# Nine key blocks instead of ten in the product with the values: the leftover 64 keys stand twice in one transposed block

## The chip, the cores and the metric

One core of a Trainium2 chip runs the whole program in one launch. The metric is the device time of that launch in microseconds (us); smaller is better. A core has five engines that run at the same time, each through its own queue in order: TensorE (PE, its weight loads shown apart as PEld), VectorE (DVE), ScalarE (ACT), GpSimd (POOL) and SyncE (SP, which here issues DMAs).

## What is computed

Three layers follow each other: a sharpened attention over 4 batches of 8 heads (576 tokens, head size 64), a gated MLP (512 to 1536 and back) and a squared-ReLU MLP (512 to 2048 and back) over the 2304 tokens. The change touches only the attention:

```python
scores = scale * np.matmul(q, k.transpose(0, 1, 3, 2))
thresh = np.max(scores, axis=-1, keepdims=True) - tau
scores = np.where(scores >= thresh, scores, -1000000000.0)
attn = np.exp(scores - np.max(scores, axis=-1, keepdims=True))
attn = attn / (np.sum(attn, axis=-1, keepdims=True) + 1e-09)
return np.matmul(attn, v)
```

## The kernel before, in words

**Number format.** Most matrix products run in a reduced format (f32r) on operands split in two: a high part (the rounded value) and a low part (what the rounding left). A product of two split operands is the sum of three or more matmuls.

**Tiles of the attention.** Queries go in tiles of 128 against all 576 keys: 9 tiles for each pair of heads, 4 pairs for each batch, 4 batches, so 144 tiles (`tiles`, `NTILE`). Two heads share the fifth tile (`ORDER`, kind "T"). The steps of a tile t are small functions, and the main loop (the last `for i in range(NTILE + lag + 1)` ahead of `at.close()`) calls the steps of several tiles in iteration i, `lag` being 2:

- `QK` (L653, PE): scores into one of two PSUM areas. `RED` (L663, DVE): row maximum less tau. `CUT` (L671, ACT): the thresholded scores into `z`. `EXP` (L679, ACT): the exponential into a tile `e` of 577 columns with its row sum; there are three `e` tiles in turn (`es`).
- `RCP` (L684, DVE) and `NORM` (L689, POOL), one iteration later: the reciprocal of the sum, and the 576 columns of `e` multiplied by it in place.
- `TR` (L711, PE), at i = t + 2: `e` is transposed by 128 x 128 matmuls with the identity, five blocks of keys for one tile. 576 keys are four blocks of 128 and one of 64. Bank `tx` takes keys 0 to 127, 128 to 255 and, as its third block, the 64 keys from 512 on; bank `ty` takes keys 256 to 383 and 384 to 511. From tile 20 on the attention has two PSUM banks for this, so tile t + 1 writes the same two banks that tile t wrote.
- `PH` (L731, ACT), at i = t + 3: the high parts, `tx` (384 columns) and `ty` (256 columns) into slots 0 to 4 of the tile `pt` (10 slots of 640 query columns). `PL` (L76, DVE): the low parts, bank less high part, into slots 5 to 9, with one subtraction for `tx` and one for `ty`. Both banks come free for the next `TR` when `PL` has read them.
- `AV` (L756, PE): the product with the values. For each pair of heads there are four products over query columns (`PARTS`: 256, 320, 320 and 256 columns, made at tiles 1, 4, 6 and 8 of the nine). Each is ten matmuls into one bank: five blocks of high parts and five of low parts, each against the 128 value rows of its block; the stationary operand has the high and the low parts of the values side by side, so that one matmul makes both products. The block of 64 keys is a full matmul whose lower 64 value rows are zero (`pack` puts zeros there), and the lower 64 rows of its block in the bank are zeroed once, by three `memset`s at the start (L432).

The first batch (`cfg["way"][0]`, letters D and K) goes another way: the transposed blocks are copied whole and the product is five plain f32 matmuls (L751, `ptf`, `vf`). It has no `PL` work. So `AV` at L756 is made for 12 pairs of heads: 48 products, and `PL` for 108 tiles.

**What else fills PE.** While the attention runs, `work(i)` gives PE matmuls of the first MLP for batches that are done (`fill_group`: L256 and L301), 12 of them in most iterations in which no product with the values is made.

**What sets the order.** Every engine takes its instructions in the order of a priority: the place at which the instruction is emitted in the program, moved up or down by `tc.high_priority(offset=...)`. `at_` takes the offset from `cfg["early"]` (from the second batch on): `TR` is moved 8 places ahead, `PL` 12 back, `NORM` 25 back, `PH` 6 ahead. In an iteration `QK` of the next tile is emitted, then `work(i)` (a product with the values, or fill), then `TR`; so the transposes stand among the last matmuls that `work(i)` emitted. The block of 64 keys has a further offset of 9 in `TR` and goes second.

The functions that the diff touches:

Of the kernel before, what the change touches and what calls it, by code (L numbers as in the profile page):

```python
# [10 lines left out]
F32 = mybir.dt.float32  # L11
F32R = mybir.dt.float32r
# [5 lines left out]
AF = mybir.ActivationFunctionType  # L18
ALU = mybir.AluOpType
# [3 lines left out]
P = 128  # L23
B, H, S, D = 4, 8, 576, 64
# [3 lines left out]
NPAIR = H // 2  # L28
# [15 lines left out]
SLOPE = 2.0**96  # L44
# [38 lines left out]
def attention_moe(tc, qkv, qk0, tau, w1, w2, out, cfg):  # L83
    nc = tc.nc
    ops = Ops(nc)
    mm = nc.tensor.matmul
# [334 lines left out]
    for j in range(LIVE):  # L421
        c0 = LAST + j * PIECE
# [5 lines left out]
    psum = p1.enter_context(tc.tile_pool(name="psum", bufs=1, space=PSUM))  # L428
    bank = [psum.tile([P, 512], F32, name=f"bank{j}") for j in range(4)]
    mp1 = Mm(bank[3:])  # L430
    for x in bank[:3]:
        nc.vector.memset(x[S - 4 * P :, 2 * P : 3 * P], 0.0)  # L432
    at = ExitStack()
    rawp = at.enter_context(tc.tile_pool(name="rawp", bufs=1, side="right"))
    qp = at.enter_context(tc.tile_pool(name="qp", bufs=2, side="right"))
    ptp = at.enter_context(tc.tile_pool(name="ptp", bufs=1, side="right"))

    es = [ptp.tile([P, S + 1], F32, name=f"e{j}", tag=f"e{j}") for j in range(cfg["lag"] + 1)]
    zs = [ptp.tile([P, S + 1], F32, name=f"z{j}", tag=f"z{j}") for j in range(cfg["zs"])]
    st_ = ptp.tile([P, S], mybir.dt.bfloat16, name="st_")  # L440
    sm = at.enter_context(tc.tile_pool(name="sm", bufs=4, side="right"))
# [7 lines left out]
    for i in range(2):  # L449
        t = [ptp.tile([P, P], F32R, name=f"qt{i}{j}", tag=f"qt{i}{j}") for j in range(2)]  # L450
# [30 lines left out]
    for h in range(4):  # L481
        c0 = 5 * 640 + h * (VW + D) + (1 - h % 2) * VW
        nc.gpsimd.memset(flat[:, c0 : c0 + D], 0.0)

    def whole(p, i):

        ways = cfg["way"][p // NPAIR % len(cfg["way"])]
        return p < NPAIR and ways[i] in "FEKD"
# [136 lines left out]
    SLOT = (0, 1, 4, 2, 3)  # L625
# [4 lines left out]
        6: (320, 320, 1, [(512, 0, 64), (256, 64, 256)]),  # L630
        8: (0, 256, 1, [(0, 0, 256)]),
    }
    pt = ptp.tile([P, 10, 640], F32R, name="pt", tag="pt")
    tiles = [(b, p, i) for b in range(B) for p in range(NPAIR) for i in range(9)]
    NTILE = len(tiles)
    st = [dict() for _ in range(NTILE + 8)]
# [38 lines left out]
    def EXP(t):  # L675
        e = es[t % len(es)]
        st[t]["e"] = e
        sum_ = sm.tile([P, 1], F32, name=f"sum{t}", tag="sum")
        ex = nc.scalar.activation(e, st[t]["z"], AF.Exp, scale=-SLOPE, accum_out=sum_)  # L679
        st[t].update(sum=sum_, exp=ex.ins)  # L680

    def RCP(t):
# [1 line left out]
        nc.vector.reciprocal(r, st[t]["sum"])  # L684

    def NORM(t):
        e = st[t]["e"][:, :S]
        r = st[t]["r"]
        norm = nc.gpsimd.tensor_scalar(e, e, scalar1=r, scalar2=1.0, op0=ALU.mult, op1=ALU.mult)  # L689
        st[t]["norm"] = norm.ins  # L690


# [4 lines left out]
    def way(t):  # L697
        b, p, i = tiles[t]
        return WAYS[cfg["way"][b % len(cfg["way"])][i]]

    def TR(t):
        e = st[t]["e"]
        tx, ty = (
            bank[(2 * t + j) % (3 if t < cfg["three"] else 2)][:, : n * P].rearrange("p (c q) -> p c q", q=P)
            for j, n in enumerate((3, 2))
        )
        for dst, cols in ((tx, ((0, 0), (2, 4 * P), (1, P))), (ty, ((0, 2 * P), (1, 3 * P)))):
            for j, c0 in cols:
                n = min(P, S - c0)
                with tc.high_priority(offset=9) if n < P else nullcontext():  # L710
                    mm(  # L711
                        dst[:n, j],
                        e[:, c0 : c0 + n],
                        ident,
                        is_transpose=True,
                        start=(j == 0),
                        stop=(j == 1),
                    )
        st[t].update(tx=tx, ty=ty)

    def halves(t):

        return ((st[t]["tx"], 0, 3, way(t)[0]), (st[t]["ty"], 3, 2, way(t)[1]))
# [8 lines left out]

    def PL(t):
        o = PTCOL[tiles[t][2]]
        for src, s0, n, how in halves(t):
            lo = pt[:, 5 + s0 : 5 + s0 + n, o : o + P]
            hi = pt[:, s0 : s0 + n, o : o + P].bitcast(F32)
            if how == "V":
                ops.sub("D", lo, src, hi)

    def AV(t):
        b, p, i = tiles[t]
        lo, n, odd, segs = PARTS[i]
        hd = heads[b * H + 2 * p + odd]
        no, o = mp1.tile()
        mr = slice(D, P) if odd else slice(0, D)
        cr = slice(0, D) if odd else slice(D, P)
        one = whole(b * NPAIR + p, i)
        if one:
            for k in range(5):  # L750
                mm(o[:, :n], hd["vf"][:, SLOT[k] * D : SLOT[k] * D + P], ptf[:, k, lo : lo + n], start=(k == 0), stop=(k == 4))  # L751
                if k < 4:
                    yield
        else:
            for k in range(10):
                mm(o[:, :n], hd["vs"][:, SLOT[k % 5], :], pt[:, k, lo : lo + n], start=(k == 0), stop=(k == 9))  # L756
        base = b * S
        out_x = [(xF[mr, p, base + dst : base + dst + w], slice(src, src + w)) for dst, src, w in segs]

        def main():  # L760
            for x_, sl in out_x:
                ops.copy("A" if not one else cfg["om"], x_, o[mr, sl])
            if one:
                end()

        def fin():
            for x_, sl in out_x:
                nc.vector.tensor_tensor(x_, x_, o[cr, sl], op=ALU.add)  # L768
            end()

        def end():
            if i == 8 and p == NPAIR - 1:
                fstate["done"] = b

        if one:
            mp1.post(no, (cfg["om"], main))
        else:
            mp1.post(no, ("A", main), ("D", fin))
# [92 lines left out]
    lag = cfg["lag"]  # L871
# [12 lines left out]
    for i in range(NTILE + lag + 1):  # L884
        mp1.age += 1
        fstate["i"] = i
        t = i - lag - 1
# [10 lines left out]
        if i < NTILE:  # L898
            at_(EXP, i)
# [3 lines left out]
        if 0 <= t < NTILE:  # L903
            at_(PL, t)
            if tiles[t][2] in PARTS:
                avq.append(t)
        if 0 <= i - 1 < NTILE:
            at_(RCP, i - 1)
            at_(NORM, i - 1)
# [5 lines left out]
        if 0 <= i - lag < NTILE:  # L915
            at_(TR, i - lag)
# [9 lines left out]
        if i < NTILE:  # L926
            b, p, k = tiles[i]
# [25 lines left out]
    f = 0  # L953
# [638 lines left out]
def pack(inputs):  # L1592
    import numpy as np

    q, k, v = (np.asarray(inputs[n]) for n in "qkv")
    qkv = np.zeros((B * NPAIR, P, RAWW), np.float32)
    qkv[:, :, 0:S] = q.reshape(B * NPAIR, 2, S, D).transpose(0, 1, 3, 2).reshape(-1, P, S)
    qkv[:, :, S : 2 * S] = k.reshape(B * NPAIR, 2, S, D).transpose(0, 1, 3, 2).reshape(-1, P, S)
    vv = v.reshape(B * NPAIR, 2, S, D)
    full = qkv[:, :, 2 * S :].reshape(B * NPAIR, P, 2, 5, D)  # L1600
    full[:, :, :, :4] = vv[:, :, : 4 * P].reshape(B * NPAIR, 2, 4, P, D).transpose(0, 3, 1, 2, 4)
    full[:, :D, :, 4] = vv[:, :, 4 * P :].transpose(0, 2, 1, 3)
    qkv[:, :, 2 * S :] = full.reshape(B * NPAIR, P, 2 * VW)

    def bits(w):
        return np.ascontiguousarray(w).view(np.int64)

    def cols(w, nf):
        return bits(w).reshape(NC, P, nf, P).transpose(2, 1, 0, 3).reshape(nf, P, DM)

    w1 = np.concatenate(
        [
            cols(inputs["moe_w_gate"], NF1),
            cols(inputs["moe_w_val"], NF1),
            bits(inputs["moe_w_out"]).reshape(NF1, P, DM),
        ],
        axis=2,
    )
    w2 = np.concatenate([cols(inputs["moe2_w_in"], NF2), bits(inputs["moe2_w_out"]).reshape(NF2, P, DM)], axis=2)
    tau = np.broadcast_to(np.asarray(inputs["tau"]).reshape(1, 1), (P, 1))  # L1620
    return [
        ("in_qkv_dram", np.ascontiguousarray(qkv)),
        ("in_qk0_dram", np.stack([np.concatenate([qkv[0, r : r + D, : 2 * S]] * 2) for r in (0, D)])),
        ("in_tau_dram", np.ascontiguousarray(tau)),
        ("in_w1_dram", np.ascontiguousarray(w1)),
        ("in_w2_dram", np.ascontiguousarray(w2)),
    ]
# [41 lines left out]
def program(arrays):  # L1669
    import concourse.bacc as bacc  # L1670

    nc = bacc.Bacc("TRN2", target_bir_lowering=False, num_devices=1, dynamic_dma_scratch_size=512)
    args = [nc.dram_tensor(n, a.shape, mybir.dt.from_np(a.dtype), kind="ExternalInput").ap() for n, a in arrays]
    out = nc.dram_tensor("out_0_dram", (NT, DM), F32, kind="ExternalOutput").ap()
    with tile.TileContext(nc) as tc:
        attention_moe(tc, *args, out, CFG)
    return nc
# [9 lines left out]
```

## Time and profile before

| what | us |
| --- | --- |
| time before, median of 3 runs | 1131.31 (1129.37 to 1132.91) |
| profiled execution, its own time | 1130.32 |
| span of that execution, first to last instruction | 1128.5 |
| PE busy | 1106.4 (98% of the span) |
| PE weight loads busy | 1007.2 (89%) |
| DVE busy | 848.8 (75%) |
| ACT busy | 677.0 (60%) |
| POOL busy | 240.6 (21%) |

The span is 1.8 us shorter than the profiled execution's own time, and that execution is 1.0 us below the median of the runs. Attention runs from the start to 418 us, together with fill; from then on only the two MLPs run. The ends of matmuls in a trace are modelled, so that a matmul of 0.12 us is drawn as 0.3 us long; the distance from one start to the next is what a matmul takes.

### The profile page before, as it was taken

To read this page: it belongs to the slowest core of one execution; us is meant where nothing else is said; L and a number is where in the kernel's file an instruction comes from. 1 tells how busy PE (TensorE), PEld (TensorE's weight loads), DVE (VectorE), ACT (ScalarE), POOL (GpSimd) and SP (SyncE) were. 2 spreads that over 40 slices of the span, in tenths; PEclk is the share of its full clock that TensorE was granted. 3 is DMA by queue.
4 is the path that set the end of the run, shared out by engine and by line. 5 is a ranking of instruction groups with operands and counts; after the bars stand their busy time and mean duration, and the time that the engine had idled before them with its cause. 6 is when DMAs were issued, how large, how long until landed. Compare 5 with 4: busy or idle time off the path is not lost.

```text
span 1128.5 us, 19599 instructions
## 1 busy us (share of the span) xinstructions
PE 1106.4 (98%) x6542; PEld 1007.2 (89%) x6542; DVE 848.8 (75%) x2088; ACT 677.0 (60%) x1593; POOL 240.6 (21%) x365
## 2 busy tenths in 40 slices
PE   7999999999999999999999999999999999999998
PEld 6788999999999999988888888888888998898887
DVE  7889987878787864889886878687568678866554
ACT  7889988988888872555434344245456455643321
POOL 5566765545455521000000000000000000000000
PEclk9999999999999999999999999999999999999999
DMA  7767645454444301222210234254355455443552
GB/s 210 218 187 197 172 118 125 113 130 119 109 108 108 76 1 47 86 94 84 76 56 20 95 129 159 95 212 180 132 195 187 168 172 183 162 160 119 193 175 78
DMA packets 60388, 148.08 MB, mean 131 GB/s; under 512 B 10240, under 2 KB 11520, under 8 KB 60288
## 3 DMA queue, kind: packets, MB, share of 16 engines
q1 hardware_dynamic: 60144, 146.83, 42.1%
q8 instruction: 52, 0.85, 0.3%
q14 instruction: 48, 0.39, 0.1%
q10 hardware_dynamic: 144, 0.00, 0.0%
HBM read 93.06 MB, written 22.28 MB: 102 GB/s over the span
## 4 chain that ended last, share of the span: by engine, by line
PE 74%; DVE 7%; ACT 5%; DMA 3%; issue 2%; POOL 0%; POOLq 0%; ACTq 0%; DVEq 0%; SPq 0%
PE mm L1497 17%; PE mm L256 16%; PE mm L1444 13%; PE mm L301 8%; PE bank L256 5%; PE bank L301 4%; PE bank L756 4%; PE bank L711 4%; PE s L653 3%; DMA wr<-in_w_dram 2%; ACT z L671 1%; DVE st__106 L663 1%; DVE pt L76 1%; ACT pt L731 1%; ACT e L679 1%
## 5 line engine op out<-in xcount | busy, mean ns | idle before, releaser
L711 PE MATMUL bank<-ident,e 128*128 128x128 f32 (+1 forms) x720 | 145.4, 276 | 3.5 <-ACT x L68 1.6
L689 POOL TENSOR_SCALAR e<-e,r 128x576 f32<-128x576 f32 x144 | 113.0, 785 | 123.7 <-DVE r L684 87.0
L76 DVE TENSOR_TENSOR pt<-bank,pt 128x384 fp32r<-128x384 f32 x216 | 100.5, 485 | 48.1 <-ACT pt L731 46.7
L256 PE MATMUL mm<-xs,wa 128*128 128x512 f32 (+2 forms) x672 | 125.8, 347 | 0.5 <-ACT x L68 0.5
L256 PEld LDWEIGHTS mm<-xs,wa 128*128 128x128 f32 x672 | 109.5, 188 | 15.7 <-ACT x L68 0.7
L671 ACT ACTIVATE z<-s,thr 128x576 f32<-128x576 f32 x144 | 106.7, 741 | 24.1 <-DVE st__106 L663 16.0
L663 DVE TENSOR_SCALAR_CACHE_REDUCE st__106<-s,tau_c 128x576 bf16<-128x576 f32 x144 | 116.8, 811 | 4.6 <-PE s L653 2.8
L256 PE MATMUL bank<-xs_m,wa 128*128 128x288 f32 x576 | 106.8, 319 | 1.6 <-DVE xF L768 0.4
L679 ACT ACTIVATE e<-z 128x577 f32<-128x577 f32 x144 | 99.4, 690 | 2.1
L711 PEld LDWEIGHTS bank<-ident,e 128*128 128x128 f32 (+1 forms) x720 | 90.9, 135 | 9.7 <-issue 3.6
L731 ACT ACTIVATE pt<-bank 128x384 fp32r<-128x384 f32 x216 | 88.5, 436 | 14.9 <-PE bank L711 13.6
L756 PE MATMUL bank<-pt,vs 128*128 128x256 f32 (+1 forms) x480 | 90.9, 318 | 0.5 <-ACT pt L731 0.2
L256 PEld LDWEIGHTS bank<-xs_m,wa 128*128 128x128 f32 x576 | 86.2, 188 | 5.2 <-DVE xs_m L76 1.9
L653 PE MATMUL s<-kh,qs 128*128 128x288 f32 x256 | 80.0, 325 | 7.4 <-DVE qs L533 5.9
L1514 DVE TENSOR_TENSOR xF<-xF,mm 128x512 f32<-128x512 f32 x54 | 37.0, 685 | 51.0 <-PE mm L1497 50.9
L256 PE MATMUL mm<-xs,wb 128*128 128x512 f32 (+1 forms) x360 | 74.9, 368 | 0.0
L756 PEld LDWEIGHTS bank<-pt,vs 128*128 128x128 f32 x480 | 72.4, 189 | 2.0 <-ACT pt L731 1.2
L653 PE MATMUL s<-kl,qs 128*128 128x288 f32 x256 | 74.1, 304 | 0.0
L68 ACT ACTIVATE wb<-wf 128x256 fp32r<-128x256 f32 x82 | 34.0, 415 | 65.4 <-DVE wf L1101 38.6
L256 PEld LDWEIGHTS mm<-xs,wb 128*128 128x128 f32 x360 | 62.9, 189 | 11.3
L1098 ACT ACTIVATE wf<-wr 128x256 f32<-128x256 f32 x64 | 27.6, 433 | 69.6 <-DMA wr<-in_w_dram 54.8
L1497 PE MATMUL mm<-wb,wx 128*128 128x512 f32 x270 | 67.1, 389 | 0.0
(156 smaller groups left out, 2535.7 us busy)
## 6 DMA issues: line engine op xcount, KB each, us to landing
wr<-in_w_dram SPq DMA_DIRECT2D x106, 256.0 KB, 3.0
raw<-in_qkv_dram SPq DMA_DIRECT2D x15, 896.0 KB, 4.7
kh<-land SPq DMA_DIRECT2D x60, 144.0 KB, 2.6
kl<-raw SPq DMA_DIRECT2D x60, 144.0 KB, 2.9
xF<-in_w_dram SPq DMA_DIRECT2D x30, 256.0 KB, 3.6
right<-kept1T SPq DMA_DIRECT2D x8, 768.0 KB, 5.6
right<-kept0T SPq DMA_DIRECT2D x7, 768.0 KB, 5.4
right<-kept SPq DMA_DIRECT2D x6, 768.0 KB, 4.5
```

The lines of the kernel that those rows point to most:

```text
L76: e.tensor_tensor(out, a, b, op=ALU.subtract)
L256: mm(pt[:, :n], w[:, a, col + c * P : col + (c + 1) * P], xs[:, b, c, :], start=(i == 0), stop=(i == len(TERMS) - 1),)
L301: mm(pt[:, :n], w[:, a, 2 * DM + m * P : 2 * DM + (m + 1) * P], u[:, b, :], start=(k == 0), stop=(k == last),)
L653: mm(sp[:, cols], l, r[:, cols], start=(n_ == 0), stop=(n_ == len(pairs) - 1),)
L663: red = nc.vector.tensor_scalar(st_, st[t]["s"][:, :S], scalar1=tau_c, scalar2=None, op0=ALU.subtract, op1=ALU.max, accum_out=th)
L671: nc.scalar.activation(z[:, :S], st[t]["s"][:, :S], AF.Prelu, bias=st[t]["thr"], scale=-1.0, alpha=1 / SLOPE)
L679: ex = nc.scalar.activation(e, st[t]["z"], AF.Exp, scale=-SLOPE, accum_out=sum_)
L689: norm = nc.gpsimd.tensor_scalar(e, e, scalar1=r, scalar2=1.0, op0=ALU.mult, op1=ALU.mult)
L711: mm(dst[:n, j], e[:, c0 : c0 + n], ident, is_transpose=True, start=(j == 0), stop=(j == 1),)
L756: mm(o[:, :n], hd["vs"][:, SLOT[k % 5], :], pt[:, k, lo : lo + n], start=(k == 0), stop=(k == 9))
L1444: mm(bank[:, :BK], w[:, a, c * P : (c + 1) * P], t[:, b, c, :], start=(n == 0 and x in ("11", "12", "S1")), stop=(n == 5), skip_group_chec ...
L1497: mm(pt, u[:, b, s * P : (s + 1) * P], w[a], start=(half == 0 and j == 0 and i == 0), stop=(half == 1 and j == 1 and i == 2),)
```

## The change

The normalised tile gets 640 columns. `EXP` writes `e` 64 columns to the right; `NORM` reads keys 0 to 319 and keys 256 to 575 and writes them next to each other from column 0 on, so that columns 256 to 383, the third block, hold keys 256 to 319 twice. The values' rows are packed to match: the fifth block of values holds keys 256 to 319, in the batches after the first in both halves. All five blocks are now full. `TR` puts the first three blocks in `tx` and the last two in `ty`, in the same order of slots as before. `PH` is unchanged, so the doubled block has high parts in all 128 rows; `PL` then replaces its lower 64 rows by the low parts. So one matmul does the high and the low part of these 64 keys, `pt` has nine slots, and each product has nine matmuls. `PL` becomes three subtractions: 256 columns, 128 columns on 64 partitions, 256 columns. The three `memset`s go.

```diff
-    for x in bank[:3]:
-        nc.vector.memset(x[S - 4 * P :, 2 * P : 3 * P], 0.0)
...
-    es = [ptp.tile([P, S + 1], F32, name=f"e{j}", tag=f"e{j}") for j in range(cfg["lag"] + 1)]
+    es = [ptp.tile([P, D + S + 1], F32, name=f"e{j}", tag=f"e{j}") for j in range(cfg["lag"] + 1)]
...
-    pt = ptp.tile([P, 10, 640], F32R, name="pt", tag="pt")
+    pt = ptp.tile([P, 9, 640], F32R, name="pt", tag="pt")
...
-        ex = nc.scalar.activation(e, st[t]["z"], AF.Exp, scale=-SLOPE, accum_out=sum_)
+        ex = nc.scalar.activation(e[:, D:], st[t]["z"], AF.Exp, scale=-SLOPE, accum_out=sum_)
...
     def NORM(t):
-        e = st[t]["e"][:, :S]
+
+        e = st[t]["e"]
         r = st[t]["r"]
-        norm = nc.gpsimd.tensor_scalar(e, e, scalar1=r, scalar2=1.0, op0=ALU.mult, op1=ALU.mult)
+        half = 5 * P // 2
+        src = bass.AP(tensor=e.tensor, offset=e.offset + D, ap=[e.ap[0], [S - half, 2], [1, half]])
+        norm = nc.gpsimd.tensor_scalar(
+            e[:, : 2 * half].rearrange("p (a c) -> p a c", a=2), src, scalar1=r, scalar2=1.0, op0=ALU.mult, op1=ALU.mult
+        )
...
-        for dst, cols in ((tx, ((0, 0), (2, 4 * P), (1, P))), (ty, ((0, 2 * P), (1, 3 * P)))):
-            for j, c0 in cols:
-                n = min(P, S - c0)
-                with tc.high_priority(offset=9) if n < P else nullcontext():
+        for dst, s0, blocks in ((tx, 0, (0, 2, 1)), (ty, 3, (0, 1))):
+            for j in blocks:
+                with tc.high_priority(offset=9) if s0 + j == 2 else nullcontext():
                     mm(
-                        dst[:n, j],
-                        e[:, c0 : c0 + n],
+                        dst[:, j],
+                        e[:, (s0 + j) * P : (s0 + j + 1) * P],
                         ident,
...
     def PL(t):
         o = PTCOL[tiles[t][2]]
-        for src, s0, n, how in halves(t):
-            lo = pt[:, 5 + s0 : 5 + s0 + n, o : o + P]
-            hi = pt[:, s0 : s0 + n, o : o + P].bitcast(F32)
-            if how == "V":
-                ops.sub("D", lo, src, hi)
+        if way(t) != "VV":
+            return
+        for src, lo, hi in (
+            (st[t]["tx"][:, :2], pt[:, 5:7], pt[:, :2]),
+            (st[t]["tx"][D:, 2], pt[D:, 2], pt[D:, 2]),
+            (st[t]["ty"], pt[:, 7:], pt[:, 3:5]),
+        ):
+            ops.sub("D", lo[..., o : o + P], src, hi[..., o : o + P].bitcast(F32))
...
-            for k in range(10):
-                mm(o[:, :n], hd["vs"][:, SLOT[k % 5], :], pt[:, k, lo : lo + n], start=(k == 0), stop=(k == 9))
+            for k in range(9):
+                chunk = (*SLOT, 0, 1, 2, 3)[k]
+                mm(o[:, :n], hd["vs"][:, chunk, :], pt[:, k, lo : lo + n], start=(k == 0), stop=(k == 8))
...
-    full[:, :, :, :4] = vv[:, :, : 4 * P].reshape(B * NPAIR, 2, 4, P, D).transpose(0, 3, 1, 2, 4)
-    full[:, :D, :, 4] = vv[:, :, 4 * P :].transpose(0, 2, 1, 3)
+    keys = np.r_[0 : 2 * P, 2 * P + D : S]
+    full[:, :, :, :4] = vv[:, :, keys].reshape(B * NPAIR, 2, 4, P, D).transpose(0, 3, 1, 2, 4)
+    full[:, :D, :, 4] = vv[:, :, 2 * P : 2 * P + D].transpose(0, 2, 1, 3)
+    full[NPAIR:, D:, :, 4] = full[NPAIR:, :D, :, 4]
```

## Rows read from the trace of the kernel before

**Rows 1.** Stretches: us, then busy us (count) of PE, PEld, DVE, ACT, POOL; clock; DMA.

```profile
100.00:140.00 40.00, 38.72 (x286) 36.56 (x286) 36.99 (x95) 39.34 (x103) 30.91 (x44) 1.00 0.63 173
140.00:418.00 278.00, 276.20 (x2108) 269.62 (x2107) 217.50 (x590) 240.46 (x599) 145.12 (x216) 1.00 0.41 102
```

**Rows 2.** Chain that ended last, three pieces: start, us (start to next start), what.

```profile
223.45 1.46 PE bank L756 x10
...
343.84 1.19 PE bank L756 x10
...
349.10 0.22 PE bank L711 x2
```

**Rows 3.** Groups by line and form, PEld: line, shapes, count | busy us, mean ns | idle.

```profile
L711 PEld LDWEIGHTS bank<-ident,e 128*128 128x128 f32 x576 | 78.8, 141 | 9.2 <-issue 3.6 <-POOL e L689 1.2 <-POOL qt L72 1.1
...
L711 PEld LDWEIGHTS bank<-ident,e 128*64 128x64 f32 x144 | 16.0, 111 | 0.4
```

**Rows 4.** PE in order of time, first batch: start us, us, line, shapes, count.

```profile
48.08 0.71 PE L711 MATMUL bank<-ident,e 128*128 128x128 f32 x5
```

**Rows 5.** Groups by line and form, DVE, columns as in rows 3.

```profile
L76 DVE TENSOR_TENSOR pt<-bank,pt 128x384 fp32r<-128x384 f32 x108 | 59.7, 553 | 39.4 <-ACT pt L731 38.2
L76 DVE TENSOR_TENSOR pt<-bank,pt 128x256 fp32r<-128x256 f32 x108 | 45.1, 418 | 8.7 <-ACT pt L731 8.5
...
L768 DVE TENSOR_TENSOR xF<-xF,bank 64x256 f32<-64x256 f32 x36 | 15.0, 416 | 3.1 <-ACT xF L68 2.3
```

**Rows 6.** In order of time: transposes right behind the subtractions, the first tile of 28.

```profile
105.51 0.88 DVE L76 TENSOR_TENSOR pt<-bank,pt 128x384 fp32r<-128x384 f32 x2
...
106.21 0.52 PE L711 MATMUL bank<-ident,e 128*128 128x128 f32 x3
```

**Rows 7.** The same, the last tile of 28, here behind a product.

```profile
384.72 0.89 DVE L76 TENSOR_TENSOR pt<-bank,pt 128x384 fp32r<-128x384 f32 x2 [0.65 <-ACT pt L731]
...
385.12 0.45 PE L756 MATMUL bank<-pt,vs 128*128 128x320 f32 x2
...
385.42 0.41 PE L711 MATMUL bank<-ident,e 128*128 128x128 f32 x2
```

**Rows 8.** An iteration with fill in place of a product, PE.

```profile
315.18 0.70 PE L256 MATMUL bank<-xs_m,wa 128*128 128x288 f32 x4
315.72 0.38 PE L711 MATMUL bank<-ident,e 128*128 128x128 f32 x2
```

**Rows 9.** In order of time: product ahead of its low parts, the first of 8.

```profile
129.12 0.85 PE L756 MATMUL bank<-pt,vs 128*128 128x256 f32 x5
...
129.99 0.88 DVE L76 TENSOR_TENSOR pt<-bank,pt 128x384 fp32r<-128x384 f32 x2
...
130.62 0.83 PE L756 MATMUL bank<-pt,vs 128*128 128x256 f32 x5
```

**Rows 10.** The same, the last of 8.

```profile
370.17 0.89 DVE L76 TENSOR_TENSOR pt<-bank,pt 128x384 fp32r<-128x384 f32 x2 [0.54 <-ACT pt L731]
370.19 1.46 PE L756 MATMUL bank<-pt,vs 128*128 128x256 f32 x10
```

**Rows 11.** Groups by line and form, POOL, columns as in rows 3.

```profile
L689 POOL TENSOR_SCALAR e<-e,r 128x576 f32<-128x576 f32 x144 | 113.0, 785 | 123.7 <-DVE r L684 87.0 <-ACT z L671 18.3 <-PE bank L711 5.6
...
L72 POOL TENSOR_SCALAR m_u<-m_th 128x288 fp32r<-128x288 f32 x30 | 13.1, 435 | 31.6 <-DVE m_th L286 29.5 <-DVE r L684 1.8
```

**Rows 12.** Line L711: what its engine waited for, in us and times.

```profile
  DVE pt L76: 1.6, 5
  POOL e L689: 1.2, 3
```

**Rows 13.** DVE in order of time, at the start.

```profile
0.89 0.45 DVE L432 MEMSET bank<- 64x128 f32 x3
3.23 0.15 DVE L522 TENSOR_SCALAR qscale<-tau_t 128x1 f32<-128x1 f32 x1 [1.89 <-DMA tau_t<-in_tau_dram]
```

## The prediction

> **What bounds the kernel now.** I read the stretches first, then the chain of waits, the groups by line and form, and the order of time around the steps that change. The stretch from 140 to 418 us, which holds most of the changed tiles, belongs to PE: busy 276 of 278 us, with ACT at 240 and DVE at 218 [rows 1]. Between 100 and 140 us it is otherwise: ACT is busy 39.3 of 40 us and DVE 37.0, so that PE is no longer alone there [rows 1]. In the chain the products with the values stand as runs of ten, 1.46 us for 320 columns and 1.19 us for 256, which makes 0.146 and 0.119 us for one matmul, and a transpose takes 0.11 us [rows 2]. So a matmul less is time less, wherever PE does not then stand waiting for DVE. A measurement of this kernel can tell about 0.3% (3.4 us) from no change.
>
> **The matmul that goes.** 12 pairs of heads have two products of 320 and two of 256 columns; each loses one matmul: 24 x 0.146 + 24 x 0.119 = 6.4 us of PE [rows 2]. This is the most that the change can give. Its other end is nothing, for a product that ends when its low parts come.
>
> **The wider third block.** Its transpose streams the same 128 columns of the identity; only its weights grow from 64 to 128 columns, a load of 141 ns in place of 111 [rows 3]. Five transposes in a row, the narrow one second, take 0.71 us with the drawn 0.27 us of the last: four distances of 0.11 us [rows 4], the same 0.11 us as the pair of full and narrow in the chain [rows 2]. Full follows full at the same distance as narrow follows full, so I take nothing; the ends are nothing and 144 x 30 ns = 4.3 us. "TensorE: Matmul & The Clock Gate" of the Trainium skill, section LDWEIGHTS (loading the stationary operand), says that a load takes time by its columns and not by its rows, an estimate of 53 ns more for 64 more columns. The trace agrees that the load grows, by 30 ns and not 53, and by that rule alone 144 loads would cost 4 to 8 us; it does not say that the load sets the distance, and the row of five speaks against it.
>
> **The third subtraction.** A subtraction of 384 columns takes 553 ns and one of 256 takes 418 [rows 5], 1.05 ns a column, so 128 columns take some 283 ns; that they lie on 64 partitions does not shorten it, since 256 columns on 64 partitions take 416 ns [rows 5]. Two in a row take 0.89 us and not 0.97 [rows 7]: each begins 0.08 us before the last ends. Before, the bank `tx` was free after 553 ns; now after 418 + 283 - 80 = 621 ns, 0.07 us later. The last subtraction ends 0.07 us later too, unless it waits for ACT anyway, as it does for 8.7 us in all [rows 5]. The ends for one tile are nothing and 418 + 283 - 553 = 148 ns, if nothing overlapped; I take 0.07 us, since the pairs overlap in the rows. "VectorE: DVE Perf Modes" of the Trainium skill, section The DRAIN you can't avoid, advises to keep the number of operations low, because the next one waits until the pipe is empty. The trace disagrees in size: 0.08 us of a subtraction overlap with the next. By the rule a tile would pay 148 ns. DVE as an engine gets 108 x 0.07 = 7.6 us more to do, on 218 of 278 us; that alone is covered.
>
> **Who waits for it: the next transposes.** The next tile's first transpose needs `tx` read, and PE's queue goes in order, so its wait holds everything behind it: the rest of the transposes, the product or fill, the next scores. In 28 of 107 tiles it starts 0.15 to 0.21 us after that subtraction ends (first and last: [rows 6, 7]; 105.51 + 0.55 to 106.21, 384.72 + 0.55 to 385.42). There is no slack in these, although the waits drawn so far are only 1.6 us [rows 12]. Each gets 0.07 us: 1.9 us. And 15 of the 28 stand behind a product. There the place of the transposes matters: `TR` is moved 8 ahead of where it is emitted, so two matmuls of ten go before it [rows 7] and four of twelve of fill [rows 8]; of nine, one will. The matmul saved is one that PE had ahead of the wait, and PE waits instead: 15 x 0.13 = 2.0 us of the 6.4 that do not come. Together 3.9 us. 8 of the 28 come directly after another of them, whose delay has moved everything behind it; I count the other 20 and take 2.8 us. Ends: nothing, and with 148 ns a tile 28 x 0.148 + 2.0 = 6.1 us.
>
> **Who waits for it: the product itself.** Before, the first five matmuls of a product needed only ACT's high parts. Now the third reads the doubled block and needs the second subtraction. In 40 of 48 products the third matmul starts after the `tx` subtraction's end anyway. In 8 it starts earlier, by 0.05 to 1.07 us (first and last: [rows 9, 10]). In five of these the lead is at most 0.20 us, 0.80 us together; each pays its lead, the 0.07, and 0.08 us from subtraction to matmul (129.99 + 0.55 to 130.62 [rows 9]): 1.55 us. The three others had five matmuls done and PE then stood waiting for the same subtraction, as in [rows 9] from 129.97 to 130.62; now two more matmuls come after the wait: 2 x 0.12 or 0.15 and 0.07 each, 1.0 us. Together 2.6 us; ends nothing, and with 148 ns 3.2 us.
>
> **Steps at nothing.** `NORM` gets 64 more columns: (785 - 435) / 288 = 1.2 ns each [rows 11], 0.08 us a tile. POOL has 145 of 278 us of work [rows 1], and transposes waited for it three times, 1.2 us in all [rows 12]; if that cover were gone, 144 x 0.08 = 11 us. What is queued behind `NORM` on POOL are the splits of the next pair and of the values, which come 0.08 us later with the same cover. `EXP` and `PH` keep their columns; no DMA is added or moved, and the packed input keeps its size. The three memsets are 0.45 us that end ahead of the first load, at 3.23 us [rows 13]: nothing.
>
> **Sum.** -6.4 + 2.8 + 2.6 = -1.0 us. Against the profiled execution's 1130.32 us that is 1129.3; that execution stands 1.0 us below the median of the runs, so against 1131.31 it is **1130.3 us**: the gain is mostly spent on waits for DVE, and nothing that can be measured is left.
>
> **Rivals.** (1) PE takes the whole gain: 1131.3 - 6.4 = **1124.9 us**. For it: PE is busy 276 of 278 us, and a PE that waits once has slack at the next tile, because ACT and DVE catch up. Against it: the 28 tiles without slack. (2) Slower: the release of `tx` is the place. If the subtractions do not overlap, it comes 0.15 us later, 6.1 us at the transposes and 3.2 us at the products; between 100 and 140 us, where DVE has 3.0 us free [rows 1] for some 14 tiles (318 us for 108 tiles, so 2.9 us each), 14 x 0.148 = 2.1 us, of which I let half show, 1.0 us. -6.4 + 6.1 + 3.2 + 1.0 = +3.9, **1135.2 us**. It eats the gain from 0.06 us a tile on (6.4 / 107) and shows as slower from 0.09. For it: nothing stands between the small pieces but a fixed cost; against it: the overlap in [rows 7]. (3) The weights' load sets the distance of the third block, by the 30 ns of [rows 3]: -1.0 + 4.3 = +3.3, **1134.6 us**; [rows 4] speak against it. This is what the rule on loads would do here, named above.
>
> **How the numbers follow.** No measurable change 0.50; the whole gain 0.27; the late release 0.16; the load 0.04; 0.03 is for the order of the queues, which shifts by one place wherever an instruction is added or taken away. Faster 0.28, same 0.52, slower 0.20. The range reaches from just above rival 1 to just below rival 2, 1125.2 to 1135.0, and holds the bounds of all waits; the forecast's own is 1128 to 1133.
>
> **What would show it.** In the profile after: 432 matmuls of products and no narrow transpose; transposes still 0.11 us apart; three subtractions a tile, the last ending 0.07 us later; more idle time of transposes and products laid to the subtraction (L76) by 3 to 5 us; the 278 us stretch shorter by about 1 us. The prediction is wrong if those waits stay as they are (then rival 1), or if DVE's time grows by more than 0.1 us a tile (rival 2).

## The result: 0.5% slower, and the profile after

| | before | after |
| --- | --- | --- |
| median | 1132.35 us (6 runs, 1129.37 to 1134.33) | 1137.63 us (6 runs, 1135.54 to 1138.63) |
| span of the profiled execution | 1128.5 us | 1136.3 us |
| last matmul of a product with the values starts | 418.0 us | 426.1 us |

The ratio is 1.0052, 95% interval 1.0038 to 1.0065. The medians differ by 5.3 us to the slower side, where 1.0 us faster was forecast and 1135.0 us was the upper end of the range. The loss lies in the attention. Its end moved by 8.1 us in the two profiled executions, whose spans differ by 7.8 us, so that the two MLPs behind it took what they took before. That these two executions lie further apart than the medians is the spread of single executions (the six of one kernel span 3 to 5 us).

The stretches of the changed kernel, columns as in [rows 1]:

```profile
100.00:140.00 40.00, 37.61 (x270) 34.73 (x269) 37.45 (x106) 38.37 (x100) 28.50 (x40) 1.00 0.57 167
140.00:418.00 278.00, 270.07 (x2025) 258.96 (x2022) 233.09 (x680) 240.61 (x595) 152.48 (x220) 1.00 0.42 106
```

In the 278 us stretch PE does 83 matmuls fewer than in [rows 1] (2025 for 2108) and its busy time falls from 276.2 to 270.1 us: it stands more. DVE's busy time rises from 217.5 to 233.1 us. The chain of waits over the same stretch says where the chain leaves PE. The heading line of the chain from 140 to 418 us (the view breaks such a line off at its end), of the kernel before, where L756 is the product with the values, L711 the transposes, L653 the scores, and L256 and L301 the fill:

```profile
by line: PE bank L256 18.1%; PE bank L756 14.8%; PE bank L711 14.3%; PE bank L301 13.7%; PE s L653 13.4%; issue 3.9%; DVE st__106 L663 3.5%; ACT z L671 2.9%; DVE pt L76 2.8%; ACT pt L731 2.5%; DVE xs_m L76 1.9%; DMA raw<-in_qkv_dram 1.7%; D
```

and of the changed kernel (L762 is the product with the values, L713 the transposes, L651 the scores, L661 the row maximum, L669 the cut, L733 the high parts):

```profile
by line: PE bank L256 11.3%; PE bank L713 10.3%; PE bank L762 9.2%; PE bank L301 8.1%; ACT z L669 8.1%; DVE pt L76 8.0%; PE s L651 7.7%; issue 7.4%; DVE st__103 L661 7.3%; ACT pt L733 5.7%; ACT e L677 2.6%; DVE m_th L286 1.8%; DVE xs_m L76 
```

Before, the five PE lines hold 74% of the chain. After, they hold 47%, and the rest goes round a ring: row maximum (3.5% to 7.3%), cut (2.9% to 8.1%), high parts (2.5% to 5.7%) and the subtractions L76 (2.8% to 8.0%), which let the next transposes in.

The groups of the steps that changed, columns as in [rows 3]:

```profile
L76 DVE TENSOR_TENSOR pt<-bank,pt 128x256 fp32r<-128x256 f32 x216 | 90.9, 421 | 36.6 <-ACT pt L733 32.3
L76 DVE TENSOR_TENSOR pt<-bank,pt 64x128 fp32r<-64x128 f32 x108 | 31.8, 294 | 1.7
L690 POOL TENSOR_SCALAR e<-e,r 128x640 f32<-128x640 f32 x144 | 119.6, 831 | 125.3 <-DVE r L682 76.3 <-PE bank L713 19.2 <-ACT z L669 9.2
L713 PEld LDWEIGHTS bank<-ident,e 128*128 128x128 f32 x720 | 91.3, 141 | 19.4 <-issue 8.9 <-POOL e L690 3.9 <-POOL wa L76 1.3
```

The normalising step grew by 46 ns (785 in [rows 11]), and five transposes in a row still take 0.71 us, as in [rows 4]:

```profile
49.48 0.71 PE L713 MATMUL bank<-ident,e 128*128 128x128 f32 x5
```

What the transposes and the products waited for. Of the line of the transposes:

```profile
  POOL e L690: 4.9, 13
  DVE pt L76: 4.0, 12
```

It was 1.6 us for the subtractions and 1.2 us for the normalising step in [rows 12]. Of the line of the products, before and after:

```profile
  DVE pt L76: 0.6, 2
```

```profile
  DVE pt L76: 4.0, 13
```

Together the transposes and the products wait 5.8 us longer for the subtractions.

The three subtractions themselves tell most. DVE in order of time, the same tile in both kernels; before, then after:

```profile
166.41 0.89 DVE L76 TENSOR_TENSOR pt<-bank,pt 128x384 fp32r<-128x384 f32 x2 [1.25 <-ACT pt L731]
```

```profile
166.58 1.19 DVE L76 TENSOR_TENSOR pt<-bank,pt 128x256 fp32r<-128x256 f32 x3 [0.39 <-ACT pt L733]
```

Two took 0.89 us; three take 1.19 us, although the columns are no more. The three durations add up to 421 + 294 + 421 = 1136 ns: there is no overlap left, and some 50 ns of gaps. Over all tiles in which nothing stands between them, the middle one starts 14 ns after the first has ended (median), and the third 31 ns after the middle one, where the second of two started 83 ns before the first ended.

### The profile page after: what moved, and what is told of

It reads as the page before. It is cut to its first block, busy times and chain, and to the rows that moved or that the text cites. A ratio compares the mean times of both kernels' runs of the same rounds, so it can differ in the third digit from the quotient of the medians.

```text
span 1136.3 us, 19628 instructions
## 1 busy us (share of the span) xinstructions
PE 1106.2 (97%) x6494; PEld 1001.1 (88%) x6494; DVE 867.8 (76%) x2193; ACT 679.3 (60%) x1593; POOL 248.6 (22%) x365
## 4 chain that ended last, share of the span: by engine, by line
PE 64%; DVE 12%; ACT 9%; issue 3%; DMA 3%; POOL 1%; POOLq 0%; ACTq 0%; DVEq 0%; SPq 0%
PE mm L256 17%; PE mm L1503 14%; PE mm L1450 11%; PE mm L301 8%; PE bank L256 4%; PE bank L301 3%; PE bank L713 3%; PE bank L762 3%; DVE pt L76 2%; ACT z L669 2%; DMA wr<-in_w_dram 2%; DVE st__103 L661 2%; PE s L651 2%; ACT pt L733 2%; ACT e L677 1%
## 5 line engine op out<-in xcount | busy, mean ns | idle before, releaser
L76 DVE TENSOR_TENSOR pt<-bank,pt 128x256 fp32r<-128x256 f32 x324 | 122.7, 379 | 38.3 <-ACT pt L733 32.3
L713 PE MATMUL bank<-ident,e 128*128 128x128 f32 x720 | 141.6, 276 | 9.1 <-DVE pt L76 3.0
L690 POOL TENSOR_SCALAR e<-e,r 128x640 f32<-128x640 f32 x144 | 119.6, 831 | 125.3 <-DVE r L682 76.3
L256 PE MATMUL mm<-xs,wa 128*128 128x512 f32 (+2 forms) x672 | 125.8, 347 | 0.5 <-ACT x L68 0.5
L256 PEld LDWEIGHTS mm<-xs,wa 128*128 128x128 f32 x672 | 109.5, 188 | 15.7 <-ACT x L68 0.7
L661 DVE TENSOR_SCALAR_CACHE_REDUCE st__103<-s,tau_c 128x576 bf16<-128x576 f32 x144 | 116.5, 809 | 5.1 <-PE s L651 4.0
L669 ACT ACTIVATE z<-s,thr 128x576 f32<-128x576 f32 x144 | 106.7, 741 | 21.1 <-DVE st__103 L661 14.1
L713 PEld LDWEIGHTS bank<-ident,e 128*128 128x128 f32 x720 | 91.3, 141 | 19.4 <-issue 8.9
L256 PE MATMUL bank<-xs_m,wa 128*128 128x288 f32 x576 | 104.7, 316 | 2.5 <-DVE xs_m L76 0.8
L733 ACT ACTIVATE pt<-bank 128x384 fp32r<-128x384 f32 x216 | 88.6, 437 | 19.2 <-PE bank L713 17.2
L762 PE MATMUL bank<-pt,vs 128*128 128x256 f32 (+1 forms) x432 | 87.6, 322 | 2.5 <-DVE pt L76 0.8
L256 PEld LDWEIGHTS bank<-xs_m,wa 128*128 128x128 f32 x576 | 84.9, 188 | 5.3 <-DVE xs_m L76 1.7
L651 PE MATMUL s<-kh,qs 128*128 128x288 f32 x256 | 80.6, 327 | 7.4 <-DVE qs L531 6.1
L256 PE MATMUL mm<-xs,wb 128*128 128x512 f32 (+1 forms) x360 | 74.9, 368 | 0.0
L651 PE MATMUL s<-kl,qs 128*128 128x288 f32 x256 | 74.3, 304 | 0.0
L256 PEld LDWEIGHTS mm<-xs,wb 128*128 128x128 f32 x360 | 62.9, 189 | 11.3
L762 PEld LDWEIGHTS bank<-pt,vs 128*128 128x128 f32 x432 | 65.8, 189 | 6.3 <-DVE pt L76 3.2
```

The source lines that it names most:

```text
L76: e.tensor_tensor(out, a, b, op=ALU.subtract)
L256: mm(pt[:, :n], w[:, a, col + c * P : col + (c + 1) * P], xs[:, b, c, :], start=(i == 0), stop=(i == len(TERMS) - 1),)
L651: mm(sp[:, cols], l, r[:, cols], start=(n_ == 0), stop=(n_ == len(pairs) - 1),)
L661: red = nc.vector.tensor_scalar(st_, st[t]["s"][:, :S], scalar1=tau_c, scalar2=None, op0=ALU.subtract, op1=ALU.max, accum_out=th)
L669: nc.scalar.activation(z[:, :S], st[t]["s"][:, :S], AF.Prelu, bias=st[t]["thr"], scale=-1.0, alpha=1 / SLOPE)
L690: norm = nc.gpsimd.tensor_scalar(e[:, : 2 * half].rearrange("p (a c) -> p a c", a=2), src, scalar1=r, scalar2=1.0, op0=ALU.mult, op1=ALU.mult)
```

## The experiments

The theory from the trace: the subtraction on the lower 64 rows runs alone on DVE, because it begins on another partition than its neighbours; the bank `tx` comes free 0.18 us later (median 732 ns after the first subtraction starts, 557 before), and the next transposes with it. The rivals: the third subtraction costs by its mere presence and place in the queue; the wider normalised tile and transposes cost; the product needs its low parts too early; any change of order moves the time.

**Upper rows.** Both halves of the doubled block hold the same keys against the same value rows, so the low parts can as well stand in the upper half.

```diff
-            (st[t]["tx"][D:, 2], pt[D:, 2], pt[D:, 2]),
+            (st[t]["tx"][:D, 2], pt[:D, 2], pt[:D, 2]),
```

> The changed kernel with the low parts of the doubled block taken in its upper 64 rows (from partition 0) in place of the lower 64 (from partition 64); both halves hold the same keys against the same value rows, so the product is the same. Theory A (the 64-row subtraction stands alone on VectorE because it starts on another partition: in the changed kernel it starts 14 ns after the one before has ended and the next one 31 ns after it, where two subtractions of before overlap by 83 ns): the overlaps come back, the first bank is free some 0.1 us earlier than the 0.73 us of the changed kernel's median tile, and the time falls by 2 to 5 us to 1132.5 to 1135.5 us. Theory B (it is the number of subtractions and their place in the queue, whatever rows they take): 1136.5 to 1138.5 us, as the changed kernel. Theory C (the wider normalised tile and transposes): 1136.5 to 1138.5 us.

Measured: 1131.26 us, ratio to before 0.9984 (0.9973 to 0.9995). Each of the five engines has the same instructions in the same order as in the changed kernel; the rows differ, and a few instructions carry other waits on semaphores (21 of the 324 subtractions do). The subtractions of the same tile, DVE in order of time:

```profile
166.23 0.94 DVE L76 TENSOR_TENSOR pt<-bank,pt 128x256 fp32r<-128x256 f32 x3 [1.17 <-ACT pt L733]
```

0.94 us in place of 1.19. The overlap is back, and with it 6.4 us (1137.63 to 1131.26), more than the 2 to 5 us expected. This decides between the theory and its first rival: presence, size and place in the queue are the same in both kernels. The waits agree. In the trace the transposes waited 1.6 us for the subtractions and the products 1.1 us, where it was 4.0 us each in the changed kernel, so 5.3 of the 6.4 us stand in these two lines:

```profile
  DVE pt L76: 1.6, 5
```

```profile
  DVE pt L76: 1.1, 4
```

The bank `tx` is free 614 ns after the first subtraction starts, and in 24 of 107 tiles the next transposes start within 0.21 us of that; in the changed kernel it was 732 ns and 35 tiles, before 557 ns and 28. In the stretch from 140 to 418 us PE is busy for 273.4 us and DVE for 222.4:

```profile
140.00:418.00 278.00, 273.38 (x2071) 265.33 (x2070) 222.40 (x685) 241.12 (x600) 151.04 (x217) 1.00 0.42 104
```

One more rival would be that operations on the lower 64 rows never overlap. A row of the changed kernel speaks against it. Two additions behind a product, of 64 and 256 columns, follow each other; both read and write rows 64 to 127 of `xF`, and both read rows 0 to 63 of a bank:

```profile
230.86 0.55 DVE L774 TENSOR_TENSOR xF<-xF,bank 64x64 f32<-64x64 f32 x2 [1.39 <-ACT xF L68]
```

They last 216 and 410 ns and take 0.55 us together, an overlap of 78 ns. This leaves that the rows of the third subtraction begin elsewhere than those of its neighbours.

**Wider tiles alone.** Two subtractions and ten matmuls again, on the new blocks:

```diff
-            (st[t]["tx"][:, :2], pt[:, 5:7], pt[:, :2]),
-            (st[t]["tx"][D:, 2], pt[D:, 2], pt[D:, 2]),
+            (st[t]["tx"], pt[:, 5:8], pt[:, :3]),
...
-            for k in range(9):
-                chunk = (*SLOT, 0, 1, 2, 3)[k]
-                mm(o[:, :n], hd["vs"][:, chunk, :], pt[:, k, lo : lo + n], start=(k == 0), stop=(k == 8))
+            for k in range(10):
+                chunk = SLOT[k % 5]
+                mm(o[:, :n], hd["vs"][:, chunk, :], pt[:, min(k, 8), lo : lo + n], start=(k == 0), stop=(k == 9))
...
-    full[NPAIR:, D:, :, 4] = full[NPAIR:, :D, :, 4]
```

> Only the wider half of the change: 640 normalised columns and five full transposes, but two subtractions (384 and 256 columns) and ten matmuls a product, as before. The low parts of the third block are overwritten by those of the fourth, and the fifth block's are read twice, so the product lacks the low parts of keys 256 to 319; the count, the sizes and the order of the steps are those of before. Theories A and B: the time of the kernel before, 1131 to 1134 us. Theory C: 1135 to 1138 us.

Measured: 1131.75 us, ratio 0.9997 (0.9984 to 1.0011), the time of the kernel before. The wider normalising step and the full third transpose cost nothing that can be measured. In another way this run is not the kernel before: both subtractions write slot 7 of `pt`, so that the second waits until the first is done. The subtractions of the same tile:

```profile
166.56 1.09 DVE L76 TENSOR_TENSOR pt<-bank,pt 128x384 fp32r<-128x384 f32 x2 [1.18 <-ACT pt L733]
```

1.09 us in place of 0.89: the bank `ty` comes free 0.2 us later, and the order is not that of before, as at least 50 of DVE's 2085 instructions and 71 of PE's 6542 stand elsewhere in their queues. None of this cost time, with ten matmuls. The bank `tx` came free as before, after 557 ns. So no cost of a late `ty` alone shows here, which points to the late `tx` in the changed kernel.

**No third subtraction.**

```diff
-            (st[t]["tx"][D:, 2], pt[D:, 2], pt[D:, 2]),
```

> The changed kernel without the subtraction on the doubled block: the low parts of keys 256 to 319 are left out and their high parts count twice; everything else (nine matmuls, 640 columns) is as in the changed kernel. If the third subtraction is the whole loss (theories A and B), the time falls below that of the kernel before by most of the 6.4 us of the saved matmuls: 1126 to 1129 us, and TensorE waits for L76 no more than before. Theory C (wider normalised tile and transposes): no lower than 1133 us.

Measured: 1128.90 us, ratio 0.9970 (0.9958 to 0.9982). The matmuls saved are worth something once the third subtraction is gone: the medians differ by 3.7 us (1132.57 to 1128.90), of 6.4 at the most. That TensorE would wait for L76 no more than before did not come: its transposes waited 3.2 us, where it was 1.6.

**Upper rows, with the 64-row subtraction 3 places ahead.**

```diff
-            ops.sub("D", lo[..., o : o + P], src, hi[..., o : o + P].bitcast(F32))
+            with tc.high_priority(offset=3) if hi.shape[0] == D else nullcontext():
+                ops.sub("D", lo[..., o : o + P], src, hi[..., o : o + P].bitcast(F32))
```

> As the run with the upper 64 rows, with the 64-row subtraction moved 3 places ahead in priority, so that no other operation should come between the first two subtractions of a tile. In the changed kernel that happens in 14 of 108 tiles and holds the first bank 0.7 us longer in each, 9.5 us together. Theory A with this second part: 1130 to 1133.5 us, some 2 us below the run with the upper rows alone. If what stands between them costs nothing: the same as that run.

Measured: 1128.23 us, ratio 0.9963 (0.9949 to 0.9977), 3.0 us below the upper rows alone and below the expected range, but not in the expected way: in 14 of 108 tiles another operation still stands between the first and the second subtraction. Such a tile of the changed kernel, DVE in order of time, where a step of the MLP (L286) comes between and the bank is held from 336.83 to some 337.94:

```profile
336.83 0.42 DVE L76 TENSOR_TENSOR pt<-bank,pt 128x256 fp32r<-128x256 f32 x1 [0.66 <-ACT pt L733]
...
337.17 0.44 DVE L286 SCALAR_TENSOR_TENSOR m_th<-m_th,bank 128x288 f32<-128x288 f32 x1
...
337.65 0.75 DVE L76 TENSOR_TENSOR pt<-bank,pt 64x128 fp32r<-64x128 f32 x2
```

What did change is the place between the second and the third subtraction: the next tile's row maximum (L661, 0.8 us) stood there in 17 tiles and stands there in 4. So the bank `ty` comes free earlier in 13 tiles. That this gives the 3.0 us is not shown: by the same edit at least 38 of DVE's and 98 of PE's instructions stand elsewhere in their queues, and in the run with wider tiles alone a row maximum stands between the two subtractions in 11 tiles, before in 3, without loss.

**The same order, lower rows.** The 64-row subtraction 3 places ahead, on the changed kernel.

> The changed kernel (64-row subtraction in the lower rows, so that nothing overlaps) with only the 64-row subtraction moved 3 places ahead. In the run with the upper rows this order took the row maximum (L661) out from between the second and the third subtraction in 13 of 17 tiles and the time fell by 3.0 us. If the order pays on its own: 1137.6 less 3 is 1134.6 us, 1133.5 to 1135.7. If the order paid only because the subtractions overlapped there, or was chance: 1136.5 to 1138.5 us.

Measured: 1135.41 us, ratio 1.0029 (1.0016 to 1.0042), 2.2 us below the changed kernel, though the two intervals overlap a little. The order pays without the overlap too. This run and the one above have the same instructions in the same order on all five engines, and only the rows differ: 1135.41 to 1128.23 is a second measure of the overlap, 7.2 us.

**Transposes 7 places ahead in place of 8**, with upper rows and the joined order.

```diff
-        "TR": 8, "LD": -21, "FD": 4, "NEG": -4, "FA": -19, "PL": -12, "PS": -25, "PH": 6, "LS": 64, "RCP": -8,
+        "TR": 7, "LD": -21, "FD": 4, "NEG": -4, "FA": -19, "PL": -12, "PS": -25, "PH": 6, "LS": 64, "RCP": -8,
```

> As the run with the upper rows and the joined order, with the transposes moved 7 places ahead of their place in place of 8, so that again two matmuls of a product go ahead of the first transpose and not one. Without any third subtraction the run stood at 1128.9 us, 2.7 us short of the 6.4 us that the saved matmuls are worth. If that is the place of the transposes, as the prediction had it (15 tiles by 0.13 us, 2.0 us): 1126 to 1127.5 us. If the place of the transposes does not matter: 1127.5 to 1129.5 us.

Measured: 1129.50 us, ratio 0.9984 (0.9970 to 0.9998). It is no faster, rather slower than with 8. The edit did what it was meant to: ahead of the transposes inside a product stand two or three matmuls (in 18 and 14 products) where it was one or two (17 and 15). The transposes' wait for the subtractions fell from 1.5 to 0.2 us, and that of the products rose from 1.2 to 3.6 us. The wait only moved.

**The doubled block last**, with upper rows and the joined order.

```diff
-            for k in range(9):
+            for j, k in enumerate((0, 1, 3, 4, 5, 6, 7, 8, 2)):
                 chunk = (*SLOT, 0, 1, 2, 3)[k]
-                mm(o[:, :n], hd["vs"][:, chunk, :], pt[:, k, lo : lo + n], start=(k == 0), stop=(k == 8))
+                mm(o[:, :n], hd["vs"][:, chunk, :], pt[:, k, lo : lo + n], start=(j == 0), stop=(j == 8))
```

> As the run with the upper rows and the joined order, with the doubled block as the last of the nine matmuls of a product in place of the third, so that the first four need only ScalarE's high parts, as five did before. The prediction priced the early need for low parts at 2.6 us for 8 products. If that holds: 1125.5 to 1127 us. If the products come late enough, or the wait only moves on to the fifth matmul: 1127.5 to 1129 us.

Measured: 1125.88 us, ratio 0.9943 (0.9929 to 0.9957): 6.2 us below the kernel before, nearly all of the 6.4 us, and the fastest of all. What the products waited for, in its trace:

```profile
  DVE pt L76: 0.8, 4
```

0.8 us for the subtractions, where it was 1.2 us without this move and 4.0 us in the changed kernel. The transposes' wait rose at the same time, from 1.5 to 3.0 us, so that these waits do not show where the 2.3 us between the two runs come from.

**The doubled block last, on the changed kernel alone.**

> The changed kernel (lower rows, order of the subtractions as it was) with only the doubled block moved to the end of the nine matmuls of a product. With the upper rows and the joined order this move took the time from 1128.2 to 1125.9 us, 2.3 us. If the early need for low parts costs that in any case, and more where the subtraction comes later: 1133.5 to 1135.5 us. If it costs only next to the other two: 1136.5 to 1138.5 us.

Measured: 1135.69 us, ratio 1.0033 (1.0024 to 1.0043), 0.2 us above the expected range and 1.9 us below the changed kernel; the two intervals overlap a little. The products' wait for the subtractions fell from 4.0 to 2.9 us; that of the transposes stayed at 4.0 us.

**All subtractions moved back by 8 in place of 12**, with upper rows and the joined order.

```diff
-        "TR": 8, "LD": -21, "FD": 4, "NEG": -4, "FA": -19, "PL": -12, "PS": -25, "PH": 6, "LS": 64, "RCP": -8,
+        "TR": 8, "LD": -21, "FD": 4, "NEG": -4, "FA": -19, "PL": -8, "PS": -25, "PH": 6, "LS": 64, "RCP": -8,
```

> As the run with the upper rows and the joined order, with all subtractions moved back by 8 places in place of 12 (few places in VectorE's order change). If what is left of the loss is VectorE's order around the subtractions: 1126 to 1127.8 us. If not: 1127.5 to 1129.5 us.

Measured: 1128.21 us, ratio 0.9961 (0.9948 to 0.9974): no different. The edit moved some 5 of DVE's instructions.

**The same on the kernel before**, meant as a measure of what a mere change of order does.

> The kernel before with its subtractions moved back by 8 places in place of 12: a few places in the queues change and nothing else. It measures what a mere change of order is worth here. If order alone moves this kernel by 2 us or more, the small steps of the other runs (2 to 3 us) can be chance: below 1130 or above 1134.5 us. If not: 1130.5 to 1134 us.

Measured: 1131.48 us, ratio 0.9990 (0.9980 to 0.9999). This does not measure what a change of order is worth: in its trace only 2 of DVE's 2085 instructions and none of PE's stand elsewhere. The run with wider tiles alone is the better control, with 50 and 71 of them moved and the time of the kernel before. One such run does not rule chance out for each of the steps of 2 to 3 us.

## Why the prediction was wrong

**The step that failed** is in the part on the third subtraction: "I take 0.07 us, since the pairs overlap in the rows". The pairs of [rows 7] overlap because both begin on partition 0. The new one begins on partition 64, and so it neither overlaps with the one before nor lets the one behind overlap. Measured, `tx` is free 0.18 us later in the median tile, 0.25 us in the mean (801 ns after the first subtraction starts, 553 before), and the last subtraction begins 0.29 us later (763 ns after the first, 475 before, where nothing stands between), where 0.07 us stood for both. Even the upper end, 148 ns "if nothing overlapped", was too small: it counted no gaps and 283 ns for a subtraction that took 294, and it took the last subtraction's delay from the same sum. With the overlap back, in the run with upper rows, `tx` is free after 614 ns and the prediction had 621; the time is 1.3 us below that of before measured beside it, and the sum had -1.0. The sum agrees with that kernel and not with this one, and in part by luck: one of its terms is not borne out, and another is missing (below).

The trace of before had the sign. An operation that adds rows of one half of a bank to rows of the other half of `xF` (L768), so that one operand begins on partition 64, stands between two subtractions there; DVE in order of time, kernel before:

```profile
373.19 0.56 DVE L76 TENSOR_TENSOR pt<-bank,pt 128x384 fp32r<-128x384 f32 x1 [0.96 <-ACT pt L731]
373.78 0.42 DVE L768 TENSOR_TENSOR xF<-xF,bank 64x256 f32<-64x256 f32 x1
374.24 0.42 DVE L76 TENSOR_TENSOR pt<-bank,pt 128x256 fp32r<-128x256 f32 x1
```

The three start 0.59 and 0.46 us apart, 0.03 and 0.04 us more than the durations, and not 0.08 us less. [rows 5] show that operation's duration, which I used; its neighbours in time are what I should have read. The Trainium skill has the rule too, in "VectorE: DVE Perf Modes", section Two Vector instructions with no wait between them: by a model there, an instruction starts only when every earlier one has finished if an input or its output begins in another group of 32 partitions than in the last instruction that read or wrote the same memory. The runs agree, with 14 and 31 ns of gap and 0.94 against 1.19 us. The section that the prediction cited points to this one; the advice on the number of operations stands further down that page of the skill, in Rules for kernel authors.

**The other steps.**

- The matmul that goes: 432 are left, as told. That 6.4 us are there to be had agrees with the fastest run (6.2 us), in which the order of other instructions differs too.
- The wider third block and `NORM`: nothing, shown by the run with wider tiles alone (0.9997). The transposes' longer wait for the normalising step (4.9 us, before 1.2) costs nothing by itself: it was 4.1 us with upper rows and 4.2 us in the kernel before with its subtractions moved, both with about the time of before. The rival by the rule on loads falls with it, and so does its mechanism, as transposes stay 0.11 us apart.
- The next transposes: right as the place, too small in size, since the release comes 0.18 us later and not 0.07. The second half of the term, that the saved matmul is one that went ahead of the wait (2.0 us), is not borne out as a cost of its own: moving the transposes back by one place took their wait to the products and gained nothing. The transposes have one matmul ahead in 17 products and still two in 14, where one was told for all. In the run without the third subtraction one matmul stands ahead in 28 products, and there the transposes did wait longer (3.2 us).
- The product itself: 2.6 us were priced for its early need of low parts. Moving the doubled block to the end gave 2.3 us with the overlap and 1.9 us without it. The size agrees. The mechanism is not shown: the waits of the products fell by 0.4 and 1.1 us only, and at least 32 of DVE's and 112 of PE's instructions changed their place with the move.
- A term that the sum did not have: the order of the queues, at which the prediction put a chance of 0.03 and no price. The row maximum stands between the second and third subtraction in 17 tiles; the runs that took it out of 13 were 3.0 and 2.2 us faster, though that the row maximum is the cause is not shown.
- Rival 2 had the place of the loss, and its sign came: DVE's time grew by 0.30 us a tile (0.89 to 1.19), more than the 0.1 us named for it. It "shows as slower from 0.09" us a tile, and it was 0.18. Its price was 3.9 us above the kernel before, and 5.3 us were measured; it had the release 148 ns late, and it was 175.

**What stays open.** Without the third subtraction 2.7 us of the 6.4 us still do not come, while the fastest run, which has all three, gets 6.2 us. The order in DVE's and PE's queues differs between the two, and no run tells which difference it is. The same holds for the steps of 2 to 3 us by order and by the place of the doubled block: the times are measured, their causes are open.

## What to carry to other kernels

An overlap of two operations in a trace belongs to that pair: before it is given to a new operation, look for a row in which a neighbour begins on the same partitions as the new one does. Where two halves of a tile are interchangeable, put the extra work into the half that begins where its neighbours do; here that alone was worth 6.4 us, as much as the saved matmuls could give at the most. And it is worth a try to use last the operand that is finished last: the two runs that moved one matmul to the end of its group were 2.3 and 1.9 us faster, though the waits do not show why.

## What the runs showed that was not expected

Moving 64 rows of one 0.3 us operation from partitions 64 to 127 to partitions 0 to 63, with every instruction in the same place of the same queue, changed the time of the whole program by 6.4 us; over 108 tiles that is 59 ns for each, out of 0.25 us that DVE loses in one of them. PE, which was busy for 99% of the stretch before, had little slack: the bank `tx` comes free 0.12 us later than with the upper rows (732 and 614 ns), and half of that shows as time.
